# An adaLN block with an S4 convolution and a spatial-gating MLP on one core: the convolution's last rounds in a written order, and the sums of w_sp a tile ahead

## Chip, cores, metric

One core of one Trainium2 chip runs the whole program. The metric is the device time of one execution in microseconds; lower is better. Times are medians of several runs. The profiled execution is one more run, with its own time.

## What is computed

x is [1, 2048, 576] in float32. Six rows of 576 come out of silu(c) @ w_mod: shifts, scales and gates for two halves.

```python
h = _layernorm(x, axis=-1) * (1 + ca) + sa
x = x + ga * _A_ref(h, A_re, A_im, B_re, B_im, C_re, C_im, log_dt, Dskip)   # S4: a causal convolution of length 2048 per channel
h = _layernorm(x, axis=-1) * (1 + cb) + sb
z = _gelu(jnp.einsum("bsd,df->bsf", h, w_in))          # 576 -> 4608
z1 = z[..., :2304]
z2 = _layernorm(z[..., 2304:], axis=-1)
g = jnp.einsum("ts,bsf->btf", w_sp, z2) + b_sp[None, :, None]
x = x + gb * jnp.einsum("bsf,fd->bsd", z1 * g, w_out)  # 2304 -> 576
```

## The kernel before

The program has three parts, traced by `ssm`, `Mlp.phase_a` and `Mlp.phase_b`. A planner (the Tile framework's scheduler) orders each engine's instructions by its own cost model, unless an instruction is *pinned*: `Pin` and `Pinned` (L119 to L139) hand every instruction to `keep_in_program_order`, which puts it behind the instruction traced just before it on its engine. `Mlp.tied` is the pinned set of engines. In the version before, `phase_a` is pinned, `ssm` and `phase_b` are not (but for the ScalarE squares in `norm_sp` and `norm_out`).

**Convolution (`ssm`).** The convolution is a two-stage transform over 5 chunks of channels, four of 128 and one of 64 (`CHW`; chunk 3 is `NC - 2`, chunk 4 is `NC - 1`). For each chunk and round: `u_load` reads the first stage's result from DRAM; `u_unit` transforms it on TensorE, ScalarE copies it out (`ue`) and two DMAs on POOL's queue make the copy with swapped halves (`us`); `z_unit` makes the kernel's spectrum on TensorE and VectorE multiplies (`za`, `zb`); `v_unit` transforms back, ScalarE copies (`v`), and POOL's queue stores to `v_d` in DRAM. When a chunk's rounds are stored, four y units follow, each for four token blocks: `y_load` reads v back by token (two loads into `u1` or `ue` buffers) and x (into `xb`, `us`, or tiles that stay), and `y_unit` does the last small transform on TensorE, adds on VectorE and stores to `x1_d` on POOL's queue. SP's queue issues all loads. The work is laid out in ticks by the dictionary `plan`, each `y_load` one tick ahead of its `y_unit`; the loop runs to `END` and, near its end, calls the MLP's `start`, `start_load` and `start_block`. Buffers: `xb`, `za`, `zb`, `v` have two each, `u1` five, `ue` and `us` four.

**The MLP's start.** `start` opens pools and loads the modulation rows (`mrow`), the tail channels of x (`x1l`) and the first four token blocks of x1 (`x1f`); it squares the rows, forms a power-of-two scale and scales the rows. A block of w_in (512 columns) is loaded by `start_load`, squared and summed by `start_sum` (ScalarE), scaled by `win_scale` (the total over partitions is a matmul with ones, then eight small VectorE steps), and split into float16 high and low parts by `start_hi` (ScalarE) and `start_lo` (VectorE). Five such blocks serve z2.

**`phase_a`.** For each of 16 tiles of 128 tokens: `ln2_stats`, `roots`, `ln2_rows` normalize a row tile two to three tiles ahead (VectorE), `turn` transposes it (TensorE), `turn_hi` and `turn_lo` split it into `nt` (ScalarE, VectorE), `z2_mm` multiplies by five blocks of w_in (TensorE, 14 matmuls a block), `z2_gelu` applies GELU (ScalarE), `z2_stats`, `roots`, `z2_norm`, `z2_hi`, `z2_lo` normalize the tile before and split it, and POOL's queue stores it. Side work is put in lists by tile and place (`side(tile, place, ...)`): w_in's other half, and for w_sp the squares in tiles 4, 6, 8 and 10 (`norm_sp`), the scale in tile 11 (`scales_sp`, at the place PE, between blocks 0 and 1) and the splits from tile 11 on. All helpers are pinned, and their instructions carry line L129.

**`phase_b`.** 4 quarters of tokens by 18 blocks of channels: `z1_unit` (14 matmuls, GELU) runs some units ahead of `g_unit` (48 matmuls with w_sp's split, gate, split of the product). After a quarter, `out_unit` multiplies by w_out: 18 x 3 matmuls for each half of the columns, pa for the high and pl for the low product. In the first quarter's units w_out is loaded and squared (`out_load`, `norm_out`), scaled (`scales_out`) and loaded again and split (`wout_load`, `wout_split`); in each quarter the next quarter's w_sp is loaded, squared, scaled and split.

Of the kernel before, what the change touches and what calls it, by code (L numbers as in the profile page):

```python
# [141 lines left out]
def ssm(tc, I, x1_d, consts_s, dram, mod_d, mlp):  # L142
# [5 lines left out]
    with ExitStack() as ctx:  # L148
# [311 lines left out]
        def part(n, bufs=2):  # L460
            return sb.tile([128, 512], F32, name=n, bufs=bufs)
# [42 lines left out]

        def y_load(c, q):
            bs = slice(4 * q, 4 * q + 4)
            w = CHW[c]
            if c == NC - 1:
                t = part("ue", 4)
                vt = [t[:, :4 * w], t[:, 4 * w:]]  # L510
            else:
                vt = [part("u1", 5)[:, :4 * w] for _ in range(2)]
            for hh in range(2):
                S.dma_start(by(vt[hh], c), v_d.rearrange("(b g r) k d -> b (g r k) d", g=4, r=2)[bs, 128 * hh:128 * hh + 128, chan(c)].rearrange("b p d -> p b d"))
            if c >= NC - 2 and q == 0:
                xb = mlp.x1f[:, :, chan(c)]
            elif c == NC - 1:
                xb = mlp.x1l[:, bs]
            else:
                xb = by(part("us", 4) if c == NC - 2 and q > 1 else part("xb"), c)  # L520
                S.dma_start(xb, I["x"][:, bs, chan(c)])
            st["y", c, q] = vt, xb, bs

        def y_unit(c, q):
            vt, xb, bs = st.pop(("y", c, q))
            w = CHW[c]
            pm = ps1()[:, :4 * w]
            for b in range(4):
                for hh in range(2):
                    T.matmul(pm[64 * hh:64 * hh + 64, w * b:w * b + w], st4[:, 4 * q + b, hh], vt[hh][:, w * b:w * b + w],  # L530
                             start=True, stop=True, skip_group_check=True)
            V.tensor_tensor(xb, by(pm, c), xb, op=ALU.add)
            G.dma_start(x1_d[bs, :, chan(c)].rearrange("b p d -> p b d"), xb)
# [8 lines left out]
        for c in range(NC):  # L542
# [12 lines left out]
        END = max(plan) + 1  # L555
        LAST_U = max(t for t in plan for f, a in plan[t] if f is u_load) + 1

# [21 lines left out]
        sb = cs = None  # L579
        for tick in range(END):  # L580
            if tick == 9:
# [112 lines left out]
class Mlp:  # L694
    def __init__(self, tc, ctx, I, x1_d, dram, mod_d, acc, out):
        self.tc, self.I, self.x1_d, self.mod_d, self.acc, self.out = tc, I, x1_d, mod_d, acc, out
        self.ctx = ctx
        self.nc, self.tied = tc.nc, Pinned(tc)
        self.win_d = dram.tile([18, 128, 10, 128], F16, name="win_d")
        self.z2_d = dram.tile([18, 128, 16, 2, 128], F16, name="z2_d")  # L700
        self.n2_d = dram.tile([4, 128, 4, 9, 128], F16, name="n2_d")
        self.wts, self.wss = {}, {}

# [34 lines left out]

    def win_scale(self, q):
# [3 lines left out]
        V.tensor_tensor(wcol(q, INV_IN), wcol(q, I_W), self.col(I_H), op=ALU.mult)  # L743

# [5 lines left out]

    def total(self, dst, c0, n, ps=None):

        nc = self.nc
        s = self.acc[:, c0:c0 + 1]
        if n > 1:
            s = self.mc.tile([128, 1], F32, name="sums")
            nc.vector.reduce_sum(s, self.acc[:, c0:c0 + n], axis=mybir.AxisListType.X)
        if ps is None:
            ps = self.ps1()
        nc.tensor.matmul(ps[:, :1], self.ones, s, start=True, stop=True)  # L760
        nc.vector.tensor_copy(dst, ps[:, :1])

    def start(self):

        nc = self.nc
        V, A, S, I = nc.vector, nc.scalar, nc.sync, self.I
        mc = self.mc = self.pool(self.ctx, "mc", 1)
# [5 lines left out]
        self.sc = mc.tile([128, 96], F32, name="sc")  # L773
        col = self.col
        wzp = self.pool(self.c2, "wzp", 1)
# [8 lines left out]
        S.dma_start(self.x1f[:, :, 384:], I["x"][:, :4, 384:])  # L784
        S.dma_start(self.x1f[:, :, :384], self.x1_d[:4, :, :384].rearrange("b p d -> p b d"))
        self.stg = self.pool(self.c2, "stg", 2)
        sq = self.stg.tile([128, 5, 512], F32, name="wst").rearrange("p a b -> p (a b)")[:, :2 * D].rearrange("p (a b) -> p a b", a=2)
        A.activation(sq[:, 0], mrow[:, 0], AF.Square, accum_out=col(T0))
        A.activation(sq[:, 1], mrow[:, 1], AF.Square)
        V.reduce_max(col(T1), sq[:, 1], axis=mybir.AxisListType.X)  # L790
        V.tensor_scalar(col(T1), col(T1), 1152.0, None, op0=ALU.mult)
        V.scalar_tensor_tensor(col(N_H), col(T0), 2.0, col(T1), op0=ALU.mult, op1=ALU.add)
        pow2_scale(V, mc, col(N_H), col(S_H), col(I_H))
        V.tensor_scalar(mrow, mrow, col(S_H), None, op0=ALU.mult)

    def start_load(self, q, pool=None):
# [12 lines left out]
    def start_lo(self, q):  # L809
# [3 lines left out]
        self.win_last(5 + q, t, w)  # L813

    def start_block(self, q):
        self.start_sum(q)
        self.win_scale(5 + q)
        self.start_hi(q)
        self.start_lo(q)

# [193 lines left out]
    def phase_a(self):  # L1014
        (self.nts, self.ns, self.xts, self.mvx, self.rx, self.tps, self.pzs, self.zs, self.bz, self.zn, self.zhl,
         self.wsp) = [{} for _ in range(12)]
        self.prods, self.z1s, self.n2, self.bsp, self.gbs, self.wfs = {}, {}, {}, {}, {}, {}
# [172 lines left out]
    def out_unit(self, q, tt):  # L1190
# [7 lines left out]
        for h in range(2):  # L1198
# [12 lines left out]
        A.dma_start(self.out[b], ot)  # L1211

    def phase_b(self):
# [5 lines left out]
        for i, (q, f) in enumerate(seq):  # L1219
# [6 lines left out]
            self.g_unit(q, f)  # L1226
            if q == 0:
                if 0 < f < 7:
                    self.norm_out(2 * f - 2)
                    self.norm_out(2 * f - 1)  # L1230
                if f < 6:
                    self.out_load(bp, 2 * f)
                    self.out_load(bp, 2 * f + 1)
                if f == 7:
                    self.scales_out(self.pb.tile([128, 512], F32, name="po", bufs=4))
                if 7 < f < 17:
                    self.wout_split(f - 8)
                if 6 < f < 16:
                    self.wout_load(f - 7)
            if q < 3:  # L1240
                if 6 < f < 15:
                    self.norm_sp(q + 1, f - 7)
                if 5 < f < 14:
                    self.wsp_load(q + 1, f - 6, bp)
                if f == 15:
                    self.scales_sp(q + 1, self.pb.tile([128, 512], F32, name="po", bufs=4))
# [77 lines left out]
```

## Time and profile before

| | us |
|---|---|
| median of 3 runs | 1928.09 |
| runs | 1928.04 to 1930.09 |
| profiled execution | 1930.98 |
| its span, first to last instruction | 1929.2 |
| TensorE busy in the span | 1820.8 |
| VectorE busy | 908.5 |
| ScalarE busy | 637.2 |

The profiled execution takes 1.8 us more than its span, and 2.9 us more than the median. PE is TensorE's matmuls, DVE VectorE, ACT ScalarE, POOL GpSimd (here only the issuer of stores), SP SyncE, the issuer of loads; a q behind an engine's name is its queue. A line of a timeline has start, length, engine, line, operation, tile written and read, shape, count, and in brackets the engine's idle time just before and what ended it.

### The profile page before, as it was taken

What the parts mean: (1) busy time and instruction counts of PE and PEld (TensorE: products, weight loads), DVE (VectorE), ACT (ScalarE), POOL (GpSimd) and SP (SyncE); (2) the same over time, 40 slices, a digit from 0 to 9 for tenths busy, and PEclk for the clock granted to TensorE, in tenths of its full rate; (3) what the DMA queues carried; (4) which work ended last, traced back from release to release, by engine and by line L of the source; (5) the groups of instructions that cost most, each with busy time, mean ns of one, the idle gap of its engine ahead of it and who ended that gap; (6) DMA issues with size and microseconds to landing.
All of it is one profiled execution on the core that took longest, in us unless ns stands there. A gap on an engine that the chain in (4) does not pass through costs nothing.

```text
span 1929.2 us, 28149 instructions
## 1 busy us (share of the span) xinstructions
PE 1820.8 (94%) x11634; PEld 936.1 (49%) x11634; DVE 908.5 (47%) x2020; ACT 637.2 (33%) x873; POOL 208.5 (11%) x317
## 2 busy tenths in 40 slices
PE   3778999995999899999999999999999999999998
PEld 1444555563444343444456444457444447444457
DVE  5887989847999872224252121252212152211221
ACT  3759999733776563111100011100001110001000
POOL 3121323331121110000000000000000000000000
PEclk9988999996999999999999999999999999999999
DMA  7667546796665456456452233451223351323211
GB/s 216 168 178 231 152 127 165 198 261 191 216 221 197 154 193 240 150 182 237 151 191 57 101 110 134 178 181 56 96 108 137 140 171 57 104 88 113 76 56 38
DMA packets 144000, 290.41 MB, mean 151 GB/s; under 512 B 20896, under 2 KB 74400, under 8 KB 133504
## 3 DMA queue, kind: packets, MB, share of 16 engines
q1 hardware_dynamic: 111744, 141.43, 24.1%
q0 software_dynamic: 29824, 142.47, 21.9%
q10 hardware_dynamic: 2304, 4.72, 0.6%
q8 instruction: 91, 1.49, 0.3%
q14 instruction: 37, 0.30, 0.0%
HBM read 219.11 MB, written 60.02 MB: 145 GB/s over the span
## 4 chain that ended last, share of the span: by engine, by line
PE 74%; DVE 4%; issue 2%; DMA 2%; ACT 1%; POOL 0%; SPq 0%; ACTq 0%; DVEq 0%; POOLq 0%
PE pg L1170 13%; PE pg L1171 13%; PE pg L1172 13%; PE pz L1158 11%; PE pz L129 9%; PE po L1204 4%; PE po L1206 4%; PE po L1205 4%; DMA u<-v_d 1%; PE po L1158 1%; PE pk L491 1%; PE pk L478 1%; DVE bsz L129 1%; DMA wf<-win_d 0%; PE pk L500 0%
## 5 line engine op out<-in xcount | busy, mean ns | idle before, releaser
L1170 PE MATMUL pg<-wsp,z2f 128*128 128x512 f16 x1152 | 437.2, 380 | 0.0
L1171 PE MATMUL pg<-wsp,z2f 128*128 128x512 f16 x1152 | 436.6, 379 | 0.0
L1172 PE MATMUL pg<-wsp,z2f 128*128 128x512 f16 x1152 | 436.6, 379 | 0.0
L1174 DVE SCALAR_TENSOR_TENSOR gt<-pg,sc,bsp 128x512 f32<-128x512 f32 x72 | 54.0, 750 | 617.5 <-PE pg L1172 617.3
L1178 ACT ACTIVATE z<-gt 128x512 f16<-128x512 f32 x72 | 45.3, 629 | 801.6 <-DVE gt L1176 801.6
L129 PE MATMUL pz<-wz,nt 128*128 128x512 f16 (+1 forms) x1120 | 243.3, 366 | 1.2 <-ACT nt L129 0.7
L1158 PE MATMUL pz<-n2q,wf 128*128 128x512 f16 (+1 forms) x924 | 218.6, 382 | 2.6 <-DMA wf<-win_d 2.6
L1170 PEld LDWEIGHTS <-z2f 128*128 128x128 f16 x1152 | 112.5, 98 | 142.2 <-issue 13.6
L1172 PEld LDWEIGHTS <-z2f 128*128 128x128 f16 x1152 | 112.7, 98 | 135.9
L1171 PEld LDWEIGHTS <-z2f 128*128 128x128 f16 x1152 | 112.7, 98 | 128.6
L129 PEld LDWEIGHTS <-nt 128*128 128x128 f16 x1120 | 106.1, 100 | 134.7 <-issue 48.8
L1158 PEld LDWEIGHTS <-wf 128*128 128x128 f16 x1008 | 97.8, 98 | 143.9 <-issue 34.2
L1204 PE MATMUL po<-wout,z 128*128 128x288 f16 x576 | 164.8, 286 | 0.0
L1205 PE MATMUL po<-wout,z 128*128 128x288 f16 x576 | 164.7, 286 | 0.0
L1206 PE MATMUL po<-wout,z 128*128 128x288 f16 x576 | 164.7, 286 | 0.0
L1166 POOL DMA_DIRECT2D z2f<-z_d x72 | 38.4, 533 | 1068.2 <-PE pg L1172 995.3
L1208 DVE TENSOR_TENSOR ot<-ot,po 128x288 f32<-128x288 f32 x32 | 14.5, 454 | 146.9 <-ACT ot L1207 146.9
L1207 ACT ACTIVATE ot<-po 128x288 f32<-128x288 f32 x32 | 13.2, 411 | 193.6 <-PE po L1206 193.6
L1179 DVE TENSOR_TENSOR gt<-gt,z 128x512 f32<-128x512 f32 x72 | 49.8, 691 | 45.1 <-ACT z L1178 45.1
L1204 PEld LDWEIGHTS <-z 128*128 128x128 f16 x576 | 56.4, 98 | 14.9 <-issue 0.7
L1205 PEld LDWEIGHTS <-z 128*128 128x128 f16 x576 | 56.4, 98 | 14.2
L1206 PEld LDWEIGHTS <-z 128*128 128x128 f16 x576 | 56.4, 98 | 14.2
(273 smaller groups left out, 2405.3 us busy)
## 6 DMA issues: line engine op xcount, KB each, us to landing
z2f<-z_d POOLq DMA_DIRECT2D x72, 1024.0 KB, 5.1
wsst<-in_w_spT SPq DMA_DIRECT2D x64, 512.0 KB, 5.0
wf<-win_d SPq DMA_DIRECT2D x72, 320.0 KB, 3.2
z_d<-zhl POOLq DMA_DIRECT2D x16, 1152.0 KB, 6.7
u_d<-st1o POOLq DMA_DIRECT2D x16, 576.0 KB, 4.0
u<-u_d SPq DMA_DIRECT2D x36, 256.0 KB, 4.9
us<-ue POOLq DMA_DIRECT2D x72, 128.0 KB, 4.5
v_d<-v POOLq DMA_DIRECT2D x36, 256.0 KB, 3.7
```

Source lines behind the costliest of these rows:

```text
L129: return self.tc.keep_in_program_order(f(*a, **k))
L1158: nc.tensor.matmul(pm.rearrange("p (t c) -> p t c", t=4), w[:p, kw], self.n2[q][:p, :, kn], start=i == 0, stop=i == len(Z1) - 1)
L1166: nc.gpsimd.dma_start(z2, self.z2_d[f])
L1170: T.matmul(pm, z2[:, st, 0], w[:, 0], start=st == 0, stop=False)
L1171: T.matmul(pm, z2[:, st, 0], w[:, 1], start=False, stop=False)
L1172: T.matmul(pm, z2[:, st, 1], w[:, 0], start=False, stop=st == 15)
L1174: V.scalar_tensor_tensor(t, pm, self.qcol(q, INV_SP), self.bsp[q], op0=ALU.mult, op1=ALU.add)
L1178: A.activation(p[:, 0], t, AF.Copy)
L1179: V.tensor_tensor(t, t, p[:, 0], op=ALU.subtract)
L1204: T.matmul(pa[:, :288], p[:, 0, ts], self.wout[:, f, 0, hs], start=f == 0, stop=False)
L1205: T.matmul(pa[:, :288], p[:, 0, ts], self.wout[:, f, 1, hs], start=False, stop=f == 17)
L1206: T.matmul(pl[:, :288], p[:, 1, ts], self.wout[:, f, 0, hs], start=f == 0, stop=f == 17)
```

## The change

Four edits.

1. **Convolution's end.** The loop over ticks stops before tick 40 (`NG + 4`). What `plan` had behind it stands written out, and all five engines are pinned from there on (`mlp.nc = mlp.tied`). In it: the z and v units of chunk 4 come ahead of the y units (2,1) to (2,3); `y_load` is taken apart into `y_vload` and `y_xload`, the nine x loads come together; y units go by token tiles (chunks 3 and 4 alternate); v loads of y units (3,0) and (3,1) go to `za` and `zb`, all x loads of chunk 3 and that of (2,3) to `us`; the sums, scales and splits of w_in's blocks 0 to 2 stand between, `start_load(2)` right behind `start`, `start_load(3)` behind y unit (3,0).
2. **The MLP's start.** `start` is cut in three: the load of x1 (`start_x1`), the squares and scale of the rows (`start_rows`, now with PSUM as scratch, a first GELU of one column behind it, and the products that `win_scale` leaves out with `inv=False`), and the rest. `ln2_stats(0)` and `roots(x=0)` move from `phase_a` in between the last y units.
3. **Sums of w_sp.** The VectorE reduction of eight partial sums leaves `scales_sp` for `sums_sp`: in `phase_a` at the end of tile 10's side work, in `phase_b` right ahead of `scales_sp`.
4. **`phase_b`.** w_out's loads, squares, scale and splits and w_sp's loads, squares and scale come one unit of 18 later. In `out_unit` the low product's matmul comes first of three, and the last token tile is stored in two halves, the second on SP's queue.

```diff
-        def y_load(c, q):
+        def y_vload(c, q):
...
+            elif c == NC - 2 and q < 2:
+                vt = [part("za"), part("zb")]
             else:
                 vt = [part("u1", 5)[:, :4 * w] for _ in range(2)]
+            st["yv", c, q] = vt
...
+        def y_xload(c, q):
...
-                xb = by(part("us", 4) if c == NC - 2 and q > 1 else part("xb"), c)
+                xb = by(part("us", 4) if c == NC - 2 or (c, q) == (2, 3) else part("xb"), c)
                 S.dma_start(xb, I["x"][:, bs, chan(c)])
...
-        for tick in range(END):
+        for tick in range(NG + 4):
...
-            if tick == NG + 5:
-                tabs.close()
-                mlp.start()
-            if tick in (NG + 7, NG + 10):
-                mlp.start_load(2 + (tick > NG + 7))
-            if tick == NG + 9:
-                mlp.start_block(2)
-            if tick in (NG + 6, NG + 7):
-                mlp.start_block(tick - NG - 6)
+        tabs.close()
+        mlp.nc = mlp.tied
+        V, A, G, T, S = mlp.nc.vector, mlp.nc.scalar, mlp.nc.gpsimd, mlp.nc.tensor, mlp.nc.sync
+        c3, c4 = NC - 2, NC - 1
+        y_load(2, 2)
+        mlp.start()
+        mlp.start_load(2)
+        mlp.start_x1()
+        for i in range(2):
+            z_unit(c4, i)
+            v_unit(c3, 6 + i)
+        mlp.start_sum(0)
+        for i in range(2):
+            z_unit(c4, 2 + i)
+            v_unit(c4, i)
+            mlp.win_scale(5 + i, False)
+            if i == 0:
+                mlp.start_sum(1)
+        v_unit(c4, 2)
+        v_unit(c4, 3)
+        for c, r in ((2, 3), (c3, 0), (c3, 1), (c3, 2), (c3, 3), (c4, 0), (c4, 1), (c4, 2), (c4, 3)):
+            y_xload(c, r)
+        y_unit(2, 1)
+        for c, r in ((2, 3), (c3, 0), (c3, 1), (c4, 0), (c4, 1)):
+            y_vload(c, r)
+        mlp.start_hi(0)
+        mlp.start_hi(1)
+        mlp.start_lo(0)
+        y_unit(2, 2)
+        y_vload(c3, 2)
+        mlp.start_sum(2)
+        mlp.win_scale(7, False)
+        mlp.start_lo(1)
+        y_unit(2, 3)
+        y_vload(c3, 3)
+        y_vload(c4, 2)
+        y_vload(c4, 3)
+        mlp.start_hi(2)
+        mlp.start_rows(ps2(), ps2())
+        mlp.start_lo(2)
+        y_unit(c3, 0)
+        mlp.start_load(3)
+        y_unit(c4, 0)
+        mlp.ap = mlp.mc
+        mlp.ln2_stats(0)
+        y_unit(c3, 1)
+        mlp.roots(x=0)
+        for c, r in ((c4, 1), (c3, 2), (c4, 2), (c3, 3), (c4, 3)):
+            y_unit(c, r)
+        mlp.nc = tc.nc
...
+    def start_rows(self, *ps):
+
+        V, A, col, mrow = self.nc.vector, self.nc.scalar, self.col, self.mrow
+        s0, s1 = [p[:, :, :D // 2] for p in ps]
+        halves = [mrow[:, i].rearrange("p (h d) -> p h d", h=2) for i in range(2)]
+        A.activation(s0, halves[0], AF.Square, accum_out=col(T0))
+        A.activation(s1, halves[1], AF.Square)
+        V.tensor_reduce(col(T1), s1, axis=mybir.AxisListType.XY, op=ALU.max)
...
+        A.activation(col(T0), self.ones[:, :1], AF.Gelu_apprx_tanh)
+        for q in range(5, 8):
+            V.tensor_tensor(self.wcol(q, INV_IN), self.wcol(q, I_W), col(I_H), op=ALU.mult)
...
+    def sums_sp(self, q):
+        self.nsp = self.sums(32 + 8 * q, 8)
+
     def scales_sp(self, q, ps=None):
...
-        self.total(col(N_S), 32 + 8 * q, 8, ps)
+        self.total(col(N_S), 32 + 8 * q, 8, ps, self.nsp)
...
+        side(10, V1, self.sums_sp, 0)
         side(11, PE, self.scales_sp, 0)
...
         for b in range(2):
-            self.ln2_stats(b)
-            self.roots(x=b)
+            if b == 1:
+                self.ln2_stats(1)
+                self.roots(x=1)
             self.ln2_rows(b)
...
+                T.matmul(pl[:, :288], p[:, 1, ts], self.wout[:, f, 0, hs], start=f == 0, stop=f == 17)
                 T.matmul(pa[:, :288], p[:, 0, ts], self.wout[:, f, 0, hs], start=f == 0, stop=False)
                 T.matmul(pa[:, :288], p[:, 0, ts], self.wout[:, f, 1, hs], start=False, stop=f == 17)
-                T.matmul(pl[:, :288], p[:, 1, ts], self.wout[:, f, 0, hs], start=f == 0, stop=f == 17)
...
+            if b == 15:
+                (A, S)[h].dma_start(self.out[b, :, hs], ot[:, hs])
+        if b < 15:
+            A.dma_start(self.out[b], ot)
...
+                if 1 < f < 8:
+                    self.norm_out(2 * f - 4)
+                    self.norm_out(2 * f - 3)
                 if 0 < f < 7:
-                    self.norm_out(2 * f - 2)
-                    self.norm_out(2 * f - 1)
-                if f < 6:
-                    self.out_load(bp, 2 * f)
-                    self.out_load(bp, 2 * f + 1)
+                    self.out_load(bp, 2 * f - 2)
+                    self.out_load(bp, 2 * f - 1)
```

More of the change, by code (lines that the diff above doesn't have):

```diff
@@ L701, in __init__ @@
         self.n2_d = dram.tile([4, 128, 4, 9, 128], F16, name="n2_d")
-        self.wts, self.wss = {}, {}
+        (self.wts, self.wss, self.nts, self.ns, self.xts, self.mvx, self.rx, self.tps, self.pzs, self.zs, self.bz, self.zn,
+         self.zhl, self.wsp) = [{} for _ in range(14)]
     def pool(self, ctx, name, bufs, **k):
@@ L749, in win_last, with sums, total @@
         self.lo(dst[:64, 9], t[:64, 4], s[:64], dst[:64, 8])
-    def total(self, dst, c0, n, ps=None):
+    def sums(self, c0, n):
+        s = self.mc.tile([128, 1], F32, name="sums")
+        self.nc.vector.reduce_sum(s, self.acc[:, c0:c0 + n], axis=mybir.AxisListType.X)
+        return s
+    def total(self, dst, c0, n, ps=None, s=None):
         nc = self.nc
[L754 to L757, printed above, removed]
+        if s is None:
+            s = self.acc[:, c0:c0 + 1] if n == 1 else self.sums(c0, n)
         if ps is None:
@@ L784, in start, with start_x1 @@
         S.dma_start(self.x1f[:, :, 384:], I["x"][:, :4, 384:])
-        S.dma_start(self.x1f[:, :, :384], self.x1_d[:4, :, :384].rearrange("b p d -> p b d"))
         self.stg = self.pool(self.c2, "stg", 2)
[L787 to L790, printed above, removed]
+    def start_x1(self):
+        self.nc.sync.dma_start(self.x1f[:, :, :384], self.x1_d[:4, :, :384].rearrange("b p d -> p b d"))
+    def start_rows(self, *ps):
[5 more added lines that the diff above has]
+        V.tensor_reduce(col(T1), s1, axis=mybir.AxisListType.XY, op=ALU.max)
         V.tensor_scalar(col(T1), col(T1), 1152.0, None, op0=ALU.mult)
         V.scalar_tensor_tensor(col(N_H), col(T0), 2.0, col(T1), op0=ALU.mult, op1=ALU.add)
-        pow2_scale(V, mc, col(N_H), col(S_H), col(I_H))
+        pow2_scale(V, self.mc, col(N_H), col(S_H), col(I_H))
         V.tensor_scalar(mrow, mrow, col(S_H), None, op0=ALU.mult)
+        A.activation(col(T0), self.ones[:, :1], AF.Gelu_apprx_tanh)
+        for q in range(5, 8):
+            V.tensor_tensor(self.wcol(q, INV_IN), self.wcol(q, I_W), col(I_H), op=ALU.mult)
     def start_load(self, q, pool=None):
@@ L813, in start_lo @@
         self.win_last(5 + q, t, w)
[L815 to L819, printed above, removed]
     def norm_sp(self, q, i):
@@ L1014, in phase_a @@
     def phase_a(self):
-        (self.nts, self.ns, self.xts, self.mvx, self.rx, self.tps, self.pzs, self.zs, self.bz, self.zn, self.zhl,
-         self.wsp) = [{} for _ in range(12)]
         self.prods, self.z1s, self.n2, self.bsp, self.gbs, self.wfs = {}, {}, {}, {}, {}, {}
```

37 lines of the change are left out of this document (20 added, 17 removed).

## The prediction

> **What bounds the kernel now.** I read the page first, then TensorE's timeline for its idle gaps, then the DMA view of the stretch with the largest gap, then VectorE's and ScalarE's timelines around each gap. After 765 us TensorE never waits again, so what the change can move lies at three places: the passage from the convolution to the MLP, one tile of the MLP's first phase, and the first units of the last phase (the tail of the program is a fourth, small one).
>
> ```profile
> span 1929.2 us, 28149 instructions
> ```
> ```profile
> 454.81 1.11 PE L530 MATMUL pk<-ue,st 128*64 128x64 f32 x14 [0.69 <-DMA ue<-v_d]
> 463.37 1.33 PE L129 MATMUL pt<-ident,n 128*128 128x128 f32 x5 [7.45 <-DVE n L129]
> ...
> 653.28 0.59 PE L129 MATMUL pz<-sums,ones 128*128 128x1 f32 x2 [6.48 <-DVE sums L129]
> 653.73 5.25 PE L129 MATMUL pz<-wz,nt 128*128 128x512 f16 x14
> ...
> 674.16 0.77 PE L129 MATMUL pt<-ident,n 128*128 128x128 f32 x5
> ...
> 689.41 0.77 PE L129 MATMUL pt<-ident,n 128*128 128x128 f32 x5
> ...
> 750.88 3.30 PE L1158 MATMUL po<-n2q,wf 128*128 128x512 f16 x14
> ...
> 760.28 4.89 PE L1158 MATMUL pz<-n2q,wf 128*128 128x512 f16 x14 [2.56 <-DMA wf<-win_d]
> ```
>
> The columns are start, length, engine, line, operation, and in brackets the idle time before and its releaser. The first row is the convolution's last y matmuls; they end at 455.9. The MLP's first transposes start at 463.37, after 7.45 us in which TensorE waits for VectorE's normalized row `n`. At 653.28 it waits 6.48 us for the sum of w_sp's squares, and the 14 matmuls behind it take 5.25 us where 14 at full clock take 3.30: the gap costs 6.48 + 1.95 = 8.4 us of TensorE's time. A tile of this phase is 689.41 - 674.16 = 15.25 us of TensorE. At 760.28 a w_in block is late: 2.56 us, and 4.89 - 3.30 = 1.6 us of slow clock.
>
> What keeps the passage long is first the transfers:
>
> ```profile
> DMA  6499999999989999999999999999999999889996
> ...
> DMA packets 19796, 15.96 MB, mean 290 GB/s; under 512 B 6598, under 2 KB 17133, under 8 KB 19793
> ...
> wst<-in_w_in SPq DMA_DIRECT2D x2, 1024.0 KB, 7.7
> ...
> mrow<-mod_d SPq DMA_DIRECT2D x1, 576.0 KB, 8.1
> ...
> x1l<-in_x SPq DMA_DIRECT2D x1, 384.0 KB, 8.6
> ```
> ```profile
> 417.25 0.37 SPq L521 DMA_DIRECT2D xb<-in_x  x1
> ```
>
> This is the DMA view of 405 to 460 us in 40 slices: nine tenths or more busy in nearly all of it. A transfer is not late here because of its own length but because of what was issued before it. SP's queue is served in order, and the x load of y unit (2,2) stands in it until 417.25, when the store of an earlier y unit frees its buffer.
>
> **The passage, part by part.** The change writes all five queues out by hand from tick 40 on. No arithmetic and no byte is removed; z, v, y, the sums and splits of three w_in blocks and their loads are moved. The new order on SP puts xload (2,2) ahead of `start`'s loads and of w_in block 2, so those wait until 417.25 (before, some went ahead). The x loads of all nine y units follow, then v loads, interleaved with y units that free their buffers. On TensorE three y units go behind the last v; on VectorE the pieces of w_in blocks 0, 1, 2 and the mod-row scaling stand ahead of the last eight y additions, and row 0's statistics and root between them.
>
> ```profile
> 417.26 0.75 DVE L790 TENSOR_REDUCE sc<-wst 128x1 f32<-128x576 f32 x1 [0.75 <-ACT wst L789]
> ...
> 419.92 0.81 DVE L794 TENSOR_SCALAR mrow<-mrow,sc 128x1152 f32<-128x1152 f32 x1
> ...
> 440.20 0.69 DVE L532 TENSOR_TENSOR zhl<-pk,zhl 128x512 f32<-128x512 f32 x1 [6.30 <-DMA xb<-in_x]
> ...
> 441.06 0.48 DVE L722 TENSOR_SCALAR wz<-wst,sc 128x512 f16<-128x512 f32 x1
> ...
> 441.58 0.74 DVE L726 SCALAR_TENSOR_TENSOR wz<-wst,sc,wz 64x512 f16<-64x512 f32 x1
> ...
> 444.35 2.34 DVE L726 SCALAR_TENSOR_TENSOR wz<-wst,sc,wz 128x2048 f16<-128x2048 f32 x1
> ...
> 455.50 2.35 DVE L726 SCALAR_TENSOR_TENSOR wz<-wst,sc,wz 128x2048 f16<-128x2048 f32 x1
> 457.76 0.42 DVE L532 TENSOR_TENSOR x1l<-pk,x1l 128x256 f32<-128x256 f32 x1
> ...
> 458.58 0.82 DVE L129 BATCH_NORM_STATS2 bsx<-zhl 128x6 f32<-128x288 f32 x2
> ...
> 463.35 0.20 DVE L129 COPY n<-n 128x64 f32<-128x64 f32 x1
> ```
> ```profile
> 429.04 0.60 ACT L502 ACTIVATE v<-pk 128x512 f32<-128x512 f32 x1 [0.63 <-DMA v_d<-v]
> 440.99 2.00 ACT L720 ACTIVATE wz<-wst,sc 128x2048 f16<-128x2048 f32 x1 [11.35 <-DVE sc L660]
> 442.90 2.32 ACT L737 ACTIVATE wz<-wst 128x2560 f16<-128x2560 f32 x1
> ```
>
> Two bounds on the new start of the MLP.
>
> (a) By the transfers. Suppose the last convolution data land no earlier than now, so the last y matmuls end at 455.9 again. Behind them stood the split of block 2 (2.35), the addition, statistics and root, and the row's own two passes. Split, statistics and root are now done earlier; left are the addition (0.42), a memset (0.3, between 457.76 + 0.42 and 458.58) and `ln2_rows` (1.8, the two 0.8 us passes and the copy that end at 463.55). The start is 455.9 + 0.42 + 0.3 + 1.8 = 458.4. The bytes speak for "no earlier, no later": 0.96 MB of `start`'s loads (576 + 384 KB) that went ahead of 417.25 now come behind it, at 290 GB/s 3.4 us more; against that four or five x1 stores, of up to 256 KB as the loads of x, now come behind the last loads, an estimated 3.5 us less.
>
> (b) By VectorE's queue. ScalarE copies the last v near 429 as now (its buffer waits for a store), then the hi parts of two blocks (2 x 2.00), then squares block 2 (2.32 + 0.2). Block 2 is issued by 417.25 plus eight issues of about 0.5, 421, and lands 7.7 later, 429, so ScalarE and not the load decides: the sum is there at 436. From there VectorE has in written order: block 2's scale (eight small steps of 0.16, from the 21 steps between 653.90 and 657.20 below, 1.3), a split (0.48 + 0.74 + 2.34 = 3.6), an addition (0.7), the mod-row chain (420.73 - 417.26 less an addition of 0.7, plus three small steps, 3.2), a split (3.6), four additions of 0.69 and four of 0.42 (4.4), statistics (1.0), root (2.1), memset and rows (2.1): 22.0. That gives 458.
>
> The two agree; I take 458.4, **5.0 us earlier** than 463.37. Everything in the MLP's first tile hangs on that transpose and moves with it. The activation-table load that moves ahead gains nothing: ScalarE waited for TensorE behind it.
>
> **Sums a tile ahead.** The reduction moves from before `scales_sp` in tile 11 to the end of tile 10.
>
> ```profile
> 647.53 0.96 DVE L129 BATCH_NORM_STATS2 bsz<-z 128x6 f32<-128x384 f32 x2
> ...
> 653.07 0.15 DVE L129 TENSOR_REDUCE sums<-acc 128x1 f32<-128x8 f32 x1
> 653.90 0.16 DVE L129 COPY sc<-pz 128x1 f32<-128x1 f32 x1 [0.68 <-PE pz L129]
> ...
> 657.20 0.55 DVE L129 BATCH_NORM_STATS2 bsz<-z 128x6 f32<-128x384 f32 x1
> 659.73 0.56 DVE L129 BATCH_NORM_STATS2 bsz<-z 128x6 f32<-128x384 f32 x1 [1.99 <-ACT z L129]
> 661.75 2.56 DVE L129 TENSOR_TENSOR zhl<-z,zhl 128x2304 f16<-128x2304 f32 x1 [1.45 <-ACT zhl L129]
> 664.22 1.01 DVE L129 TENSOR_TENSOR nt<-pt,nt 128x512 f16<-128x512 f32 x2
> ...
> 698.49 1.02 DVE L129 TENSOR_TENSOR nt<-pt,nt 128x512 f16<-128x512 f32 x2
> ...
> 714.58 1.02 DVE L129 TENSOR_TENSOR nt<-pt,nt 128x512 f16<-128x512 f32 x2
> ```
> ```profile
> 651.44 2.31 ACT L129 ACTIVATE z<-z,nm,r 128x2304 f32<-128x2304 f32 x1 [3.92 <-DVE nm L129]
> ...
> 659.01 0.69 ACT L129 ACTIVATE z<-pz,sc 128x512 f32<-128x512 f32 x1 [5.26 <-PE pz L129]
> ```
>
> TensorE was ready at 653.28 - 6.48 = 646.8. VectorE is behind it: it would reach the moved reduction just ahead of the statistics at 647.5, so a wait of some 0.9 us is left. But the tempting answer, 8.4 us, is not what comes out. The ninth of the fourteen matmuls of each tile's block 0 is the first to need the low half of `nt`, and VectorE writes `nt` every (698.49 - 664.22)/2 = 17.1 us, more than TensorE's 15.25. VectorE sets the pace here, and TensorE's lead runs out by tile 15. So count VectorE's gain in tile 11: the reduction and its wait go (653.90 - 653.07 = 0.8); the GELU that ScalarE did at 659.01 can follow the normalization at 653.75 and ends at 654.4, so the 1.99 and the 1.45 go. 0.8 + 2.0 + 1.5 = 4.3: `nt` of tile 12 at 659.9 instead of 664.22. TensorE, without its stall, would start tile 12's matmuls near 659.9 and reach those that need `nt` at 661.8, no wait; tile 13's `nt` (677.0 + 0.6) is late by about 0.7, tile 14's by 1.9, tile 15's by 0.9. The end of the phase moves by VectorE's **4.3 us**; the phase behind it starts from TensorE's last tile and VectorE's last split, both earlier by that.
>
> The clock is a small risk here: 2.56 us of idleness slowed the next 14 matmuls by 1.6 us at 760.28, and the new waits are 0.7 to 1.9. If one of them did the same, TensorE would lose 1.6 us ahead of a tile in which it waits for VectorE anyway, so at most 1.6 is lost, behind the last. The Trainium skill (TensorE: Matmul & The Clock Gate, "Why this matters for your kernels") asks for no idle gap over about 3 us; by that rule none of the new waits costs anything, though the row at 760.28 shows the loss behind 2.56 us already.
>
> **Last phase.** Loads and norms of w_out, w_sp's norms and scales come one unit later. TensorE waits nowhere there behind 765 us, so I cost that at nothing; its cover is TensorE's unbroken queue of g units, and if a split of w_out came too late the first out unit would wait for one load and split, some 5 us. At the start of the phase the late w_in block costs 4.2 us (2.56 + 1.6). SP's queue is not pinned there, and the planner puts any load whose buffer is free into SP's idle time, so one unit of program order should not move the w_out loads away: gain 0, bounds 4.2 either way.
>
> **Tail.**
> ```profile
> 1925.64 0.34 ACTq L1211 DMA_DIRECT2D out<-ot  x1
> ```
> The low product is finished two matmuls earlier (0.2 us), the last store is half as large: from its issue to the end of the span are 3.6 us, most of them not its bytes. Between 0.1 and 1.0; **0.3** taken, near the low end. The Trainium skill (DMA: Bandwidth & Descriptors, "Anatomy of one DMA", fitted on GpSimd's path) gives a DMA about 2.0 us fixed plus bytes at 436 GB/s, by which half of 288 KB less is an estimated 0.3 us for the store; no row here separates the two.
>
> **Sum.** 5.0 + 4.3 + 0.3 = 9.6. The profiled execution took 1930.98 us around its span of 1929.2, so it would take 1921.4; the runs' median of 1928.09 becomes 1918.5.
>
> **Rivals.**
> 1. The w_in block at 760.28 comes in time as well, because the first two w_out loads leave SP's queue ahead of it. For: transfers are what is late there. Against: the unpinned queue. Time: 1918.5 - 3.5 = 1915.0 (not the full 4.2, since g's own operand comes in the same crowd).
> 2. The passage stays where it is: the crowd of transfers, pushed behind 417.25, lands 5 us later, and the transposes start near 463. For: the DMA strip has no room. Against: the x1 stores that move behind. Time 1918.5 + 5.0 = 1923.5.
> 3. VectorE catches up and TensorE keeps all of its 8.4 us: 1914.4. Against: the 17.1 us beat.
> 4. The moved reduction lands too late in VectorE's queue to help, so the change does not do what it says: 1922.8.
> 5. Slower: SP's written order makes block 2 of w_in late, and with it ScalarE's square, the scale on TensorE in front of y unit (2,3), VectorE's whole chain of 22 us, and the v loads that wait for that unit's buffer. Each us behind 433.5 (when ScalarE is ready for it) is a us at the start of the MLP; equal to before as a whole when the block lands 433.5 + 9.6 = 443, slower by over 0.2% at 447. A landing at 450 gives 1928.09 + 7 = 1935. Against: 290 GB/s moves it by about 430.
>
> **Numbers.** Forecast 0.56 (1915.5 to 1921.5 by its own terms), rival 1 0.13, rival 2 0.14, rival 3 0.06, rival 4 0.04, rival 5 0.07. This kernel's runs tell about 0.2% (3.9 us) from no change. Faster by more: the forecast, 1, 3, 4 and half of 2, 0.86; within: the other half of 2, 0.07; slower: 0.07. The range of 8 in 10 reaches down to a part of rivals 1 and 3 together and up to rival 2 with 2 us more; it leaves out rival 5: 1911.5 to 1925.5.
>
> **What would show it.** Right: first `pt` transposes near 458.4; the wait for `sums` down from 6.48 to about 1; new waits of TensorE for `nt` in tiles 13 to 15 with a sum near 3.5; the late `wf` unchanged. Wrong: no waits for `nt` and 8 us gained between the first transposes and the last phase; transposes at 463 or later with TensorE's y units waiting for `v_d` to the end; w_in block 2 landing behind 435.

## The result, and the profile after

The changed kernel took 1921.28 us (median of 6 runs, 1920.77 to 1924.12) against 1930.12 us for the kernel before (6 runs, 1928.04 to 1934.96). The medians lie 8.8 us apart; the ratio is 0.9956 (95% interval 0.9942 to 0.9970), which is 8.5 us. The forecast was 1918.5 us, 9.6 us faster.

The profiled execution after spans 10.0 us less. The page's first line, and its chain of work that ended last:

```profile
span 1919.2 us, 28165 instructions
...
PE 67%; DVE 7%; issue 4%; ACT 3%; DMA 2%; POOL 1%; DVEq 0%; ACTq 0%; POOLq 0%
```

TensorE's timeline after, at the places that the prediction named (columns as there):

```profile
447.04 1.97 PE L129 MATMUL pk<-u,st 128*64 128x128 f32 x16 [5.98 <-DVE zhl L129]
...
455.13 1.33 PE L129 MATMUL pt<-ident,n 128*128 128x128 f32 x5 [3.19 <-DVE n L129]
457.14 5.42 PE L129 MATMUL pz<-wz,nt 128*128 128x512 f16 x14 [0.69 <-ACT nt L129]
...
639.30 0.38 PE L129 MATMUL pz<-sums,ones 128*128 128x1 f32 x2 [0.89 <-DVE sums L129]
639.55 3.28 PE L129 MATMUL pz<-wz,nt 128*128 128x512 f16 x14
...
669.40 4.80 PE L129 MATMUL pz<-wz,nt 128*128 128x512 f16 x20 [0.69 <-DVE nt L129]
...
683.70 1.90 PE L129 MATMUL pz<-wz,nt 128*128 128x512 f16 x8 [0.70 <-ACT nt L129]
686.53 4.80 PE L129 MATMUL pz<-wz,nt 128*128 128x512 f16 x20 [0.93 <-DVE nt L129]
...
702.60 13.00 PE L129 MATMUL pz<-wz,nt 128*128 128x512 f16 x62 [0.65 <-DVE nt L129]
715.54 3.30 PE L1221 MATMUL pz<-n2q,wf 128*128 128x512 f16 x14
...
739.04 3.30 PE L1221 MATMUL po<-n2q,wf 128*128 128x512 f16 x14 [0.82 <-DMA wf<-win_d]
742.58 3.30 PE L1221 MATMUL po<-n2q,wf 128*128 128x512 f16 x14 [0.24 <-DMA wf<-win_d]
750.05 5.73 PE L1221 MATMUL pz<-n2q,wf 128*128 128x512 f16 x14 [4.17 <-DMA wf<-win_d]
755.72 0.39 PE L1233 MATMUL pg<-wsp,z2f 128*128 128x512 f16 x1
```

The wait for `n` fell from 7.45 to 3.19 us, the wait for `sums` from 6.48 to 0.89, with no slow clock behind it (3.28 for 14 matmuls). Three places with waits for `nt` are new, of 0.69, 1.63 and 0.65 us. The late w_in block got worse: 0.82 + 0.24 + 4.17 us of waits, and 5.73 us for the 14 matmuls behind.

In the passage TensorE's waits for data from `v_d` shrink from 11.7 us in eight waits (432 to 455 us, before) to 0.9 us in two. Its long waits are now one of 8.38 us for ScalarE's square of block 2, which ends at 433.51, and one of 5.98 us for VectorE. VectorE's timeline shows its queue from the scale of block 2 to row 0, and below that the four writes of `nt` in tiles 12 to 15:

```profile
434.13 0.16 DVE L129 COPY sc<-pk 128x1 f32<-128x1 f32 x1 [0.72 <-PE pk L129]
...
442.86 2.35 DVE L129 SCALAR_TENSOR_TENSOR wz<-wst,sc,wz 128x2048 f16<-128x2048 f32 x1
...
446.31 1.01 DVE L129 TENSOR_TENSOR zhl<-pk,zhl 128x512 f32<-128x512 f32 x2
...
455.10 0.19 DVE L129 COPY n<-n 128x64 f32<-128x64 f32 x1
...
651.52 1.01 DVE L129 TENSOR_TENSOR nt<-pt,nt 128x512 f16<-128x512 f32 x2
668.65 1.02 DVE L129 TENSOR_TENSOR nt<-pt,nt 128x512 f16<-128x512 f32 x2
685.78 1.02 DVE L129 TENSOR_TENSOR nt<-pt,nt 128x512 f16<-128x512 f32 x2
701.85 1.02 DVE L129 TENSOR_TENSOR nt<-pt,nt 128x512 f16<-128x512 f32 x2
```

No bracket follows the first row up to 455.10: VectorE works 21 us without a gap. The beat of `nt`, the time from one of these writes to the next, is still 17.13 us (668.65 - 651.52).

One pair of profiles is not enough here. The program's first part already differs. A ScalarE copy in the convolution's steady rounds, ahead of the first reordered tick, shows it (ScalarE's timeline, the kernel before and then after):

```profile
396.63 0.63 ACT L422 ACTIVATE kab<-pk 128x256 f32<-128x256 f32 x1 [0.41 <-PE pk L419]
```
```profile
393.19 0.62 ACT L422 ACTIVATE kab<-pk 128x256 f32<-128x256 f32 x1 [0.41 <-PE pk L419]
```

3.44 us of the ten were there before anything had changed. So every kernel below is read by stages, each the difference of the starts of two rows: this copy, the first `pt` transposes, the first z1 unit (`n2q,wf`), the first g unit (`z2f`). The last column reaches from TensorE's end to the end of the span.

| kernel | copy at | to transposes | to first z1 | to first g | tail |
|---|---|---|---|---|---|
| before | 396.63 | 66.74 | 264.89 | 36.85 | 5.5 |
| before, second profile | 397.43 | 65.18 | 264.54 | 38.65 | 5.5 |
| before, third | 395.01 | 65.30 | 264.49 | 38.62 | 5.5 |
| sums alone | 397.45 | 65.64 | 260.59 | 38.49 | 5.5 |
| after | 393.19 | 61.94 | 260.41 | 40.18 | 4.6 |
| after, second profile | 394.15 | 62.06 | 260.51 | 39.37 | 4.5 |
| passage alone | 394.07 | 62.26 | 263.69 | 39.50 | 4.5 |
| after, last phase as before | 396.98 | 62.24 | 260.49 | 39.44 | 4.6 |
| block 2's split later | 394.91 | 60.41 | 261.86 | 37.47 | 4.6 |
| loads held back | 393.38 | 62.23 | 260.38 | 32.34 | 4.5 |
| splits spread | 392.72 | 61.95 | 257.28 | 36.25 | 4.5 |
| both | 395.27 | 62.38 | 257.85 | 33.25 | 4.5 |
| both, tile 0 reordered | 396.49 | 59.70 | 261.67 | 33.36 | 4.5 |

The stretch from the first g unit to TensorE's end is 1158.6 to 1158.9 us in nearly all of them, 1160.3 with the splits spread.

### The profile page after: what moved, and what is told of

It reads as the page before. It is cut to its first block, busy times and chain, and to the rows that moved or that the text cites. A ratio compares the mean times of both kernels' runs of the same rounds, so it can differ in the third digit from the quotient of the medians.

```text
span 1919.2 us, 28165 instructions
## 1 busy us (share of the span) xinstructions
PE 1814.3 (95%) x11634; PEld 934.3 (49%) x11634; DVE 908.5 (47%) x2020; ACT 636.4 (33%) x874; POOL 207.9 (11%) x317
## 4 chain that ended last, share of the span: by engine, by line
PE 67%; DVE 7%; issue 4%; ACT 3%; DMA 2%; POOL 1%; DVEq 0%; ACTq 0%; POOLq 0%
PE pg L1233 13%; PE pg L1234 13%; PE pg L1235 13%; PE pz L1221 11%; PE pz L129 4%; PE po L1267 3%; PE po L1268 3%; PE po L1269 3%; DVE bsz L129 1%; ACT zhl L129 1%; DMA wsst<-in_w_spT 1%; PE po L1221 1%; DMA wf<-win_d 1%; PE pk L491 1%; DVE nt L129 1%
```

## The experiments

**The changed kernel again, and the kernel before twice more**, all unaltered.

> The changed kernel once more, unaltered. It shows what moves from one execution to the next without any edit. If the 3.4 us that the first 150 us of the program gained are chance in the landing of transfers, this trace shows another amount there (anything from 0 to 4 us against the kernel before); if they belong to the change, 3.4 again. The same holds for the late w_in block at the first units of the last phase (4.17 us against 2.56): chance, or again 4 to 5 us. Time 1921.3, within 2 us.

> The kernel before once more, unaltered. Two numbers of its first profile are to be seen again. First the late w_in block at the start of the last phase: if 0.25 + 2.56 us is the kernel's own, the same again; if it was a lucky landing, 4 to 6 us, as in all profiles since (4.5 to 5.4). Second the stretch of 70 to 120 us, where the two kernels without the new order (the one before and the one with the sums alone) stand 0 and +0.8 us and the four with it 1.7 to 3.4 us ahead: chance puts this run anywhere between, a systematic cause within 1 us of the first profile.

> The kernel before a third time, for the place of the last kab copy (396.6 and 397.4 us in its first two profiles; 392.7 to 394.9 in six of the seven kernels with the new order, 397.0 in the seventh) and the stretch from there to the first transposes (66.7 and 65.2). By chance alone 393 to 397; if the new order itself is the cause, 396.5 to 397.5.

Measured: 1922.98 us after (7 runs) against 1930.77 before (24 runs), ratio 0.9967 (0.9955 to 0.9978). The kernel before against itself gave 0.9998 (0.9982 to 1.0013), and the single execution 1929.29. The copy of the table stands at 395.0 to 397.4 in three executions of the kernel before and at 393.2 and 394.2 in two of the one after, so the first profiles' 3.44 us is not the size of anything in the change. The waits for `wf` of the second profile before:

```profile
753.32 3.30 PE L1158 MATMUL po<-n2q,wf 128*128 128x512 f16 x14 [0.26 <-DMA wf<-win_d]
759.81 6.06 PE L1158 MATMUL pz<-n2q,wf 128*128 128x512 f16 x14 [3.19 <-DMA wf<-win_d]
```

With the slow clock behind that is 6.2 us, where the first profile had 4.4. The first pair's 3.3 us at this place (40.18 - 36.85) is mostly a favourable first profile: against the other two, both profiles after give 0.7 to 1.6 us.

**Each part alone.** First the sums, in the kernel before; then the passage, by putting the reduction back in the kernel after.

```diff
+        side(10, V1, self.sums_sp, 0)      # kernel before, sums alone
         side(11, PE, self.scales_sp, 0)
```
```diff
-        side(10, V1, self.sums_sp, 0)      # kernel after, passage alone
+        side(11, PE, self.sums_sp, 0)
         side(11, PE, self.scales_sp, 0)
```

> The kernel before, with only the reduction of w_sp's sums moved from tile 11 to the end of tile 10. Theory (VectorE's 17.1 us beat sets the pace of tiles 11 to 15): 4.3 us faster than the kernel before, the wait for sums down from 6.5 to about 0.9, and about 3 us of new waits for nt in tiles 13 to 15. Rival (TensorE keeps all of its stall): 8.4 us faster and no wait for nt. Second rival (the gain is given back at the first units of the last phase, where a w_in block lands by its own clock): 0 to 2 us faster, the wait for wf 2 to 4 us longer.

> The changed kernel with the reduction of the sums back in tile 11: the passage alone. Theory: the two parts add up, so 4.3 us slower than the changed kernel, about 1925.5, or 5 us faster than the kernel before; the wait for sums is 6.5 us again. Rival (the transfers of the last phase set its start): within 2 us of the changed kernel, the wait for wf shrinking by what the sums cost.

Measured, against 1930.77 us before: sums alone 1926.48 (ratio 0.9983, 0.9973 to 0.9993), 4.3 us faster; passage alone 1925.65 (0.9982, 0.9971 to 0.9992), 5.1 us faster. By medians the parts give 9.4 us, the whole 7.8 on the same chip; by the ratios they give 3.3 and 3.5 us, the whole 6.4. Both sums agree within the scatter of the runs. The table says the same more finely: the sums take 3.9 us out of the stage between transposes and first z1 unit without the new passage (264.5 to 260.6), 3.2 with it (263.7 to 260.5). The sums alone show the new waits as well (TensorE's timeline):

```profile
647.41 0.38 PE L129 MATMUL pz<-sums,ones 128*128 128x1 f32 x2 [0.89 <-DVE sums L129]
...
694.66 4.80 PE L129 MATMUL pz<-wz,nt 128*128 128x512 f16 x20 [0.93 <-DVE nt L129]
...
757.43 4.80 PE L1165 MATMUL pz<-n2q,wf 128*128 128x512 f16 x14 [3.96 <-DMA wf<-win_d]
```

So TensorE does not keep its 8.4 us, and the gain is not given back at the w_in block: the stage to the first g unit is 38.49, as in the kernel before.

**The last phase's side work one unit earlier**, as before: `norm_out(2 * f - 2)`, `out_load(bp, 2 * f)` and so on in `phase_b`, everything else as changed.

> The changed kernel with the last phase's side work (loads, norms and splits of w_out, loads and norms of w_sp) back one unit earlier, where the kernel before has it. Theory (SP's queue is not bound to the program's order there, so one unit of it moves nothing): the time of the changed kernel within 2 us, and 4.5 to 5.5 us of waits for wf. Rival (the one unit makes the w_in block late): 2 to 3 us faster, waits of 2.8 us.

Measured: 1922.55 us (ratio 0.9957, 0.9942 to 0.9973), stage to the first g unit 39.44, waits for `wf` of 1.58 and 3.73 us as in the second profile after (1.58 and 3.65). The moved side work costs and brings nothing that these runs can tell, as forecast.

**VectorE's queue in the passage.** The split of block 2 (3.6 us) goes behind row 0.

```diff
         mlp.start_rows(ps2(), ps2())
-        mlp.start_lo(2)
...
                 self.x1_load(4)
+                self.start_lo(2)
                 self.turn_lo(0)
```

> The changed kernel with the low split of w_in block 2 (3.6 us of VectorE) taken out of the queue ahead of row 0 and put into VectorE's idle time behind it, ahead of the first subtraction of nt. Theory (VectorE's unbroken queue from 434 to 455 us sets the start of the MLP): the first pt transposes come 3 to 3.6 us earlier, and since VectorE idles 2.0 and 1.6 us in tile 0 the gain stays: 2.5 to 3.6 us faster than the changed kernel, about 1918. Rival (the last v loads set it, by which 455 was 458.4 less the early program's 3.4): no change in the transposes' start, 0 us. Second rival (VectorE's work comes back as a wait in tiles 0 to 2): transposes earlier, phase not, 0 to 1 us.

Measured: 1921.14 us (0.9956, 0.9941 to 0.9972), 1.8 us below the 1922.98 of the changed kernel on the same chip, where 2.5 to 3.6 were expected. The transposes come 1.7 us closer (60.41), not 3.6, and 1.4 us of that is lost again before the first z1 unit (261.86). TensorE's timeline shows why, and below it a row of VectorE's the new hole in its queue:

```profile
449.13 1.01 PE L129 MATMUL pk<-ue,st 128*64 128x64 f32 x13 [0.35 <-DMA ue<-v_d]
...
470.93 0.59 PE L129 MATMUL pz<-acc,ones 128*128 128x1 f32 x2 [5.42 <-ACT wz L129]
```
```profile
451.99 0.69 DVE L129 TENSOR_TENSOR us<-pk,us 128x512 f32<-128x512 f32 x1 [1.28 <-PE pk L129]
```

VectorE's queue is the bound, but the last v loads stand only 1.7 us behind it: in this run the chain of waits to row 0 goes from a load of `ue` (issued at 442.46, 6.63 us to landing) over TensorE's last y matmuls to VectorE's last addition, where after VectorE had no gap from 434.13 on. Most of the 1.7 us came back as a longer wait for the sum of block 4 in tile 0 (5.42 us, after 2.66). The stages thus gain 0.3 us; the rest of the 1.8 is within the scatter, and the profiled execution also had no slow clock at the late w_in block (last section).

**The late w_in block.** SP's loads for the g units may issue only behind the load of the tenth w_in block.

```diff
+        while done < 10:
+            self.z1_unit(*seq[done])
+            done += 1
+        with self.tc.issue_after(self.last_wf.ins):
+            self.units(seq, done, bp)      # the old loop over g units
```

> The changed kernel with SP's loads for the g units of the last phase (w_out, w_sp) held behind the load of the tenth w_in block. Theory (that block is late because of the transfers that the planner puts ahead of it): the waits for wf fall from about 5 us to under 1, with them the slow clock behind (2 us): 4 to 7 us faster than the changed kernel, about 1916. Rival (what comes late then is z2f or w_out, and TensorE waits for those): within 2 us of the changed kernel, with a new wait of 3 to 5 us behind 750 us. Second rival (the z2 stores of the last tiles and not SP's loads fill the queues): no change in the waits.

Measured: 1917.33 us (0.9930, 0.9911 to 0.9949), 5.2 us below the 1922.55 of the same chip's run above, whose kernel differs from the changed one only in the side work. TensorE no longer waits between the first z1 unit and the first g unit:

```profile
738.63 6.53 PE L1221 MATMUL po<-n2q,wf 128*128 128x512 f16 x28
745.10 3.30 PE L1221 MATMUL pz<-n2q,wf 128*128 128x512 f16 x14
748.33 0.39 PE L1233 MATMUL pg<-wsp,z2f 128*128 128x512 f16 x1
```

SP's timeline explains it, first after, then with the loads held back:

```profile
732.21 2.22 SPq L888 DMA_DIRECT2D wsst<-in_w_out  x2
735.02 0.61 SPq L1207 DMA_DIRECT2D wf<-win_d  x1
735.68 0.46 SPq L1247 DMA_DIRECT2D wost<-in_w_out  x1
738.25 0.33 SPq L1207 DMA_DIRECT2D wf<-win_d  x1
```
```profile
732.24 6.78 SPq L1207 DMA_DIRECT2D wf<-win_d  x3
739.11 0.87 SPq L888 DMA_DIRECT2D wsst<-in_w_out  x2
```

The tenth `wf`, the last that TensorE needs ahead of the first g unit, is issued at 738.25 in the one and by 739.02 in the other. Held back were two loads of 432 KB and one of 576 ahead of it, and one of 1152 KB (`n2q`) 0.4 us behind it. With them it took 11.75 us, as the chain of waits after has it, and 3.0 without (by the DMA view):

```profile
738.25 11.75 DMA wf<-win_d
```

These loads are not the whole of it. In the kernel with the splits spread (the next experiment) the same three loads stand ahead of the tenth `wf`, which is issued at 734.68, and `n2q` behind it, and yet it lands in 7.7 us. One difference there is the time of the two loads of `z2f`, 1024 KB each, which POOL's queue issues beside its stores. The first one, after and then with the splits spread:

```profile
738.77 0.56 POOL L1229 DMA_DIRECT2D z2f<-z_d  x1 [7.26 <-DMA wf<-win_d]
```
```profile
740.15 0.57 POOL L1230 DMA_DIRECT2D z2f<-z_d  x1 [9.53 <-DMA wf<-win_d]
```

It comes 0.5 us behind the tenth `wf` in the one and 5.5 us behind it in the other. With the loads held back it comes at 738.91, as early as after, and TensorE does not wait. So the block was late in the profiles where both groups of loads came together; no run moved the loads of `z2f` alone, so their share is not shown.

**The splits of w_sp spread** over tiles 11 to 15.

```diff
-            side(11 + i // 2, V1, self.wsp_lo, 0, i)
+            at = (11, 12, 13, 13, 14, 14, 15, 15)[i]
+            side(at, V1, self.wsp_lo, 0, i)      # hi and load move with it
```

> The changed kernel with the eight splits of w_sp spread over tiles 11 to 15 (1, 1, 2, 2, 2) and not 11 to 14 (2 each). It takes 1.4 us of VectorE's work out of tile 11 and as much out of tile 12. Theory (VectorE's beat of 17.1 us in tiles 11 to 14 sets the pace): the waits for nt in tiles 13 to 15 (0.69 + 0.70 + 0.93 + 0.65 = 3.0 us) go, and the last phase starts 2.5 to 3 us earlier against the first transposes. Rival (the last phase's w_in blocks land by their own clock): the start earlier, the waits for wf longer by as much, 0 us in all. Second rival (the waits come from ScalarE or the new splits at the end of tile 15): start of the last phase unchanged.

Measured: 1918.89 us (0.9933, 0.9915 to 0.9951), 3.7 us below 1922.55. The stage to the first z1 unit is 257.28, 3.2 us less, and only one wait for `nt` is left:

```profile
672.91 14.83 PE L129 MATMUL pz<-wz,nt 128*128 128x512 f16 x70
...
699.03 13.00 PE L129 MATMUL pz<-wz,nt 128*128 128x512 f16 x62 [0.66 <-DVE nt L129]
...
748.21 0.39 PE L1234 MATMUL pg<-wsp,z2f 128*128 128x512 f16 x1 [2.53 <-DMA z2f<-z_d]
```

VectorE's work in tiles 11 and 12 was what held TensorE: the beat of `nt` from tile 12 to 13 and to 14 falls from 17.13 to 15.81 us. ScalarE's hi parts moved along with the splits, but ScalarE had waited 5.5 to 6.6 us for VectorE (`nm`) in each of tiles 12 to 15, so it was not the bound. The first rival fell too: the stage behind did not grow but shrank, from 39.4 to 36.25, as the tenth w_in block came in 7.7 us and no slow clock followed (waits for `wf` of 0.85 and 0.35 us). So the profile's gain has two parts of 3.2 us, of which the stretch behind the first g unit gives 1.7 back. `z2f` is late there: the last z store, behind VectorE's last splits, issues 17.4 us after the first z1 unit, where it was 14.8.

**Both together, and tile 0 reordered on top.** The second kernel adds the later split of block 2, and moves `win_scale(9)`, `start_hi(4)` and `start_lo(4)` behind `z2_mm(0, 2)`.

> The changed kernel with two of the edits tried together: the loads for the g units held behind the tenth w_in block, and the w_sp splits spread over tiles 11 to 15. The stretch from the first transposes to the first z1 unit was 260.4 us and 257.3 with the spread; the stretch from there to the first g unit 39.4 us and 32.3 with the loads held back. Theory (the two are independent): 257.3 and 32.3, 1192 us from the first z1 unit to TensorE's end, so 10 us faster than the changed kernel, about 1912 to 1913. Rival (the w_in blocks land by the clock of the transfers, so what the spread gains is waited for again): 257.3 and 35, about 1915.

> The kernel of the two edits together, with the split of w_in block 2 behind row 0 as tried before, and TensorE's matmul for the sum of w_in block 4 moved behind the first tile's third product. The split alone brought the transposes 1.7 us closer (60.4 us behind the last kab copy and not 62.1) and lost it in a wait of 5.4 us in tile 0 (2.7 before). Theory (that wait is TensorE's place in the order: the sum of block 4 stands ahead of a product that needs only block 2): transposes at +60.4, the wait under 3 us, first z1 unit within 256 us of the transposes; 2 to 3.5 us faster than the two edits alone. Rival (VectorE's work of tile 0 is the bound, in whatever order): transposes earlier, z1 not, 0 us.

Measured against 1929.71 us before: both 1912.95 us (0.9906, 0.9891 to 0.9922), the fastest of all; with tile 0 reordered 1914.57 (0.9919, 0.9905 to 0.9934), 1.6 us slower where 2 to 3.5 faster were expected. The stages of the first are 257.85 and 33.25, so the two edits add up, less a wait of 0.87 us for `z2f`. In the second the transposes come 2.7 us closer and the stage behind grows by 3.8 (TensorE's timeline):

```profile
471.81 0.38 PE L129 MATMUL pz<-acc,ones 128*128 128x1 f32 x2 [2.30 <-ACT wz L129]
...
481.53 1.01 PE L129 MATMUL pz<-wz,nt 128*128 128x256 f16 x4 [6.20 <-ACT wz L129]
```

The wait for the sum went down to 2.30 as meant, but now the hi part of block 4 is 6.20 us late, because the scale it needs stands behind row 2's work in VectorE's queue. TensorE's order was not the only cause; VectorE's was the other, as the rival had it.

## Why the prediction was right, and where it was not

**Passage (forecast 5.0).** Right in kind. The transposes start at 455.13; corrected by the 3.44 us of the program's first part that is 4.8 us earlier, and bound (b) gave the chain: 434.13 to 455.29 is 21.2 us where 22.0 were counted. It began 1.6 us later than counted (434.13 + 3.44 = 437.6, not 436), since ScalarE's last copy of v came later, so the end fits in part by luck. That the two bounds lie close is shown by the split moved later, 1.7 us. The size is off by the one profile from which it was taken: 66.74 was the longest of the four executions with the old order (the others 65.2 to 65.6), and by medians (65.47 of these four, 62.23 of the seven profiles with the written order and the split of block 2 in its place) the passage gives 3.2 us. Counted from the copy, the forecast put the transposes at 458.4 - 396.63 = 61.8 us, within 0.5 us of what came; 1.3 of the 1.8 us that are missing lie in the profile of before. Rival 2 (the crowd of transfers keeps it at 463) and rival 5 fell: TensorE waited for VectorE at 447.04, and ScalarE began the square of block 2 without waiting for its load (`wst`), right behind the two hi parts:

```profile
427.26 3.88 ACT L129 ACTIVATE wz<-wst,sc 128x2048 f16<-128x2048 f32 x2
431.05 2.32 ACT L129 ACTIVATE wz<-wst 128x2560 f16<-128x2560 f32 x1
```

**Sums a tile ahead (forecast 4.3).** Right step by step: a wait of 0.89 us is left where 0.9 was counted; `nt` of tile 12 moved by 664.22 - 651.52 = 12.70, of which 8.24 is the transposes' own shift, so 4.5; the new waits are 0.69, 1.63 and 0.65 where 0.7, 1.9 and 0.9 were worked out. The stage gave 4.1 us by medians (264.54 to 260.45). Rivals 3 and 4 fell. The Trainium skill's bound on idle gaps (TensorE: Matmul & The Clock Gate, "Why this matters for your kernels", about 3 us) agrees with the new waits: behind 0.89 us the next 14 matmuls took 3.28. It does not fit the row at 760.28 before, where 14 matmuls took 4.89 us behind 2.56 us of idleness; the measurement decides.

**Last phase (forecast 0, bounds 4.2 either way).** The first pair showed 3.3 us lost. Against three profiles of the kernel before and the sums alone (median 38.55), the five with the new passage and neither loads nor splits of w_sp moved (two executions after, passage alone, last phase as before, block 2's split later) have a median of 39.44: 0.9 us lost, inside the bounds. The cause of these 0.9 is open. It is not the moved side work, by its experiment. A w_in block that TensorE waited 0.2 to 0.6 us for with the old passage is waited for 0.8 to 1.6 us with the new, unless the loads are held back. Rival 1 (that the block comes in time) did not happen, though holding the loads back shows that it can.

**Tail (forecast 0.3, bounds 0.1 to 1.0).** 0.9 to 1.0 us, at the upper bound. The last store, as the DMA view shows it, before and then after:

```profile
out<-ot ACTq DMA_DIRECT2D x1, 288.0 KB, 2.1
```
```profile
out<-ot SPq DMA_DIRECT2D x1, 144.0 KB, 1.8
```

That is 0.3 us, as much as the Trainium skill's byte term had for the difference (DMA: Bandwidth & Descriptors, "Anatomy of one DMA"). Its whole sum, an estimated 2.7 and 2.3 us, is more than the 2.1 and 1.8 measured; it is fitted on another path than these two queues. The low product's earlier end gives 0.2 to 0.3; the remaining 0.4 lies between the store's landing and the end of the span, which the prediction did not split.

**Sum.** By the medians of the stages 3.2 + 4.1 - 0.9 + 1.0 = 7.4 us; the medians of the runs gave 8.8 and 7.8, their ratios 8.5 and 6.4. The mechanisms of the two large terms were right. The step that failed is the size of the passage, 5.0 where 3.2 were measured: it was sized from one profile of the kernel before, at the far end of a scatter of 1.6 us. In the first pair the 3.4 us of the start and the 3.3 us of the last phase, neither of them foreseen, nearly cancelled, and the profile's 10.0 us looks closer to the forecast of 9.6 than its parts are. That closeness is luck.

## What to carry to other kernels

When a stall on one engine is removed, count what the other engine's beat allows, not the stall: 8.4 us of TensorE's time were worth 4.1, and another 3.2 came only when VectorE's work was spread over more tiles. A place where two bounds agree (here VectorE's queue and the last loads) gives little to whoever relieves only one of them. And an effect of a few microseconds should be sized from stages of several executions of the kernel before, since one profile's stage can be 1.5 us off and its start 2 us.

## What was not expected of the hardware

The same idle time did not always bring the slow clock. Two executions waited 3.65 us for the same block after the same 28 matmuls; the first is the second profile after, the second the kernel with the later split of block 2:

```profile
740.99 6.53 PE L1221 MATMUL po<-n2q,wf 128*128 128x512 f16 x28 [1.58 <-DMA wf<-win_d]
751.17 4.99 PE L1221 MATMUL pz<-n2q,wf 128*128 128x512 f16 x14 [3.65 <-DMA wf<-win_d]
```
```profile
741.25 6.53 PE L1221 MATMUL po<-n2q,wf 128*128 128x512 f16 x28 [1.38 <-DMA wf<-win_d]
751.42 3.30 PE L1221 MATMUL pz<-n2q,wf 128*128 128x512 f16 x14 [3.65 <-DMA wf<-win_d]
```

4.99 us for the next 14 matmuls in one, 3.30 in the other; the granted clock over them was 0.65 and 1.00. The other profiles point the same way: behind 2.56 us of waiting they took 4.89 us, behind 3.19 6.06, behind 3.96 4.80. The length of the gap alone does not decide it.

The place of the copy near 395 us also leaves a question. It stands at 395.0 to 397.5 in the four executions with the old order and at 392.7 to 397.0 in the nine with the new one, 394.6 on average, although the new written order begins behind it. Chance can do that; whether the change has a part in it was not settled.
